# Value matmuls of two neighbouring query tiles in one TensorE visit, with the global keys' part as 32-row tiles

## The chip, the core and the metric

The kernel runs on one core of one Trainium2 chip. The metric is the device time of one execution in microseconds, as the median of several runs; smaller is better. A profile of one execution is read beside it. In the profile PE is TensorE, PEld its weight loads, DVE is VectorE, ACT is ScalarE, POOL is GpSimd and SP is SyncE, whose queue issues nearly all DMAs.

## What is computed

A sparse attention is followed by a feed-forward layer. There are 8 batches of 8 heads with a head size of 64. Each batch has 512 local queries and 32 global ones. A local query sees the 32 global keys and the local keys within 32 positions; a global query sees everything. The attention's 8 x 544 rows of 512 go through a two-layer network with an inner width of 2048 and an ELU between.

```python
s_g = scale * np.matmul(q_g, k_all.transpose(0, 1, 3, 2))        # global queries, all keys
out_g = np.matmul(sm(s_g), v_all)
mask = np.abs(pos[:, None] - pos[None, :]) <= window             # window = 32
s_ll = np.where(mask, s_ll, -1000000000.0)
s_l = np.concatenate([s_lg, s_ll], axis=-1)                      # global keys, local keys
a_l = sm(s_l)
out_l = np.matmul(a_l, np.concatenate([v_g, v_l], axis=2))
...
h = x @ w_in
g = np.where(h > 0.0, h, alpha * (np.exp(np.minimum(h, 0.0)) - 1.0))
return (g @ w_out).astype(np.float32)
```

## The kernel before

**Two streams on one core.** `attention()` and `ffn_stream()` are Python generators, and the loop at L858 interleaves them while the program is written out. Each `yield` of the attention is one step. `pace` (L845, from the table PACE) says how many chunks of the feed-forward layer stand in front of a step: none in the first 66 steps (the lead), about four a step up to step 112, about three a step after. A chunk is six matmuls of 256 columns in 16-bit parts. Work written with `defer(n, fn)` comes n ticks later, a tick being a chunk or a step without one. A planner then orders each engine's instructions by its own estimate of when they can run, taking program order as priority; waits and buffers are set by it.

**Attention.** A batch has two groups g of four heads and four tiles t of 128 local queries. The list `slots` has for each batch one slot "g" per group (global queries' scores, `stage_ga`) and eight slots "l" (g, t), in the order of two neighbouring tiles of group 0, then of group 1, and so on. In iteration i of L823 four steps are made, in the order S, V, T, U: S scores slot i (`stage_s`), V is `stage_v` of slot i - 3, T and U are `stage_t` and `stage_u` of slot i - 2. T transposes the softmaxed local scores of four heads into PSUM and copies them into `ptw` (two buffers, alternating); U transposes the scores against the global keys and copies them into `ptg` (one buffer for tile 0, another for all other tiles), and it copies the transposed scores of the global queries beside the local ones.

**The value matmuls (`stage_v`, L748).** For each of four heads three float32 matmuls add up in PSUM: the global keys (L767, 160 columns, the weights being `vG`, which holds the head's 32 global values in its own 32 rows of 128 and zeros elsewhere), and two windows of local keys (L769 and L771, 96 columns each). Two heads share the columns of one PSUM bank, on its lower and upper 64 partitions; both pairs of heads of one tile lie in one bank. A float32 matmul is two records in the trace, so that a visit has 24. After it ScalarE copies the local queries' part to `xr` (L775); one tick later VectorE adds the global queries' part to `xglob` (L780 for tile 0, L782 otherwise) and takes the maximum of the 256 new columns of `xr` (L784). When a block of 256 tokens is complete it is put into `ready`, and `split_x` cuts it into two 16-bit halves for the feed-forward layer.

**PSUM.** There are eight banks: `ps_h` two, `ps_o` two, `ps_a` four. The lead's V uses `ps_h`; later V, and S (two banks), `stage_ga` (two), T, U and `all_max` all use `ps_a`. Once the feed-forward layer has turned to its seven-product form (`ffn2_seven`, L398), that form keeps two banks of `ps_o`, one of `ps_h` and one of `ps_a` (L401 to L403) to the end, so that the attention has three banks of `ps_a` left, and `ffn1` one of `ps_h`.

**Loads.** All go through SP's queue in the program's order. `loads(i + 2)` is issued at the top of iteration i; for an "l" slot it brings q once and the tile's values `v` (384 KB, three buffers), for a "g" slot qg and k. A load into a buffer that is still read holds up the loads queued behind it.

Of the kernel before, what the change touches and what calls it, by code (L numbers as in the profile page):

```python
# [10 lines left out]
F32 = mybir.dt.float32  # L11
# [3 lines left out]
ALU = mybir.AluOpType  # L15
AX = mybir.AxisListType
# [6 lines left out]
P = 128  # L23
NT = SL // P
# [7 lines left out]
NP = NFT // 2  # L32
LAG2 = 2
LAGT, LAGV = 2, 3
AHEAD = 2


# [6 lines left out]
NX = 4  # L44
# [9 lines left out]


@with_exitstack
def attn_ffn(ctx: ExitStack, tc: tile.TileContext, qT, qgT, kT, vT, w_in, w_out, mask, out):
    nc = tc.nc
    scale = 1.0 / math.sqrt(D)

# [40 lines left out]
    make_identity(nc, ident)  # L101


    ptw = [wts.tile([P, 2, 4 * (HQ + 32) + 32], F32, name=f"ptw{i}") for i in range(2)]
# [186 lines left out]
    def ffn_stream():  # L291
# [203 lines left out]
        def split_x(blk):  # L495
            xr, mx = ready[blk]
            xh = ffn.tile([P, NC, BLK], F16, name="xh", bufs=NX)
            xl = ffn.tile([P, NC, BLK], F16, name="xl", bufs=NX)
            done = []
            xf, hf, lf = (a.rearrange("p c t -> p (c t)") for a in (xr, xh, xl))  # L500

            def s1():
                all_max(mx[:, 1:2], mx[:, 0:1])

            def s2():
                nc.vector.tensor_scalar_max(mx[:, 1:2], mx[:, 1:2], LOW)
# [12 lines left out]
            return xh, xl, mx, done  # L519
# [75 lines left out]


    def new_x():
        return ffn.tile([P, NC, BLK], F32, name="xr", bufs=3), ffn.tile([P, 10], F32, name="xm", bufs=NX + 4)

    xglob, mglob = wts.tile([P, NC, BLK], F32, name="xglob"), wts.tile([P, 10], F32, name="mglob")  # L600

    def attention():
        np_ = [0]
# [12 lines left out]
        def load_qg(b, g):  # L616
            qg = apool.tile([P, 2, SG], F32, name="qg", bufs=1)
            nc.sync.dma_start(qg, qgT[b, g])
            return qg

        def load_v(b, g, t):
            v = apool.tile([P, 12, D], F32, name="v", bufs=3)
            nc.sync.dma_start(v, vT[b, g, t])
            return v

# [110 lines left out]
        def stage_t(st, g, t):  # L736

            n = tiles[0]
            tiles[0] += 1
            pt, pz = st["pt", g, t] = ptw[n % 2], ptg[t == 0]  # L740
            tp = ps_a.tile([P, 512], F32, name="pa")
            for h in range(4):
                nc.tensor.transpose(tp[:, h * P:(h + 1) * P], st["p", g, t][:, h, 0:P], ident)  # L743
            copy = nc.vector.tensor_copy if "f" in tab or lead[0] else nc.scalar.copy
            copy(pt[:, :, 32:].rearrange("p a (h x) -> p a h x", h=4)[:, :, :, 0:HQ],
                 tp.rearrange("p (h a q) -> p a h q", h=4, a=2))

        def stage_v(st, g, t):  # L748

            half = t // 2  # L750
            blk = 2 * st["b"] + half
            if (g, t % 2) == (0, 0):
                st["x", half] = new_x()
            xr, mx = st["x", half]
            v = st["v", g, t]
            pt, pz = st["pt", g, t]
            if lead[0]:
                pv = ps_h.tile([P, 2, BLK], F32, name="h").rearrange("p a b -> p (a b)")
            else:
                pv = ps_a.tile([P, 512], F32, name="pa")  # L760
            for j in range(2):
                for i in range(3):
                    for r in range(2):
                        h = 2 * j + r
                        at = j * PW
                        if i == 0:
                            w, x, o = v[:, 8 + h, :], pz[:, 0:GW], slice(at, at + GW)  # L767
                        elif i == 1:
                            w, x, o = v[:, h, :], pt[:, 0, 32 + 96 * h:128 + 96 * h], slice(at, at + 96)  # L769
                        else:  # L770
                            w, x, o = v[:, 4 + h, :], pt[:, 1, 96 * h:96 + 96 * h], slice(at + HQ, at + GW)  # L771
                        nc.tensor.matmul(pv[64 * r:64 * r + 64, o], w, x, start=i == 0, stop=i == 2)  # L772
            pv = pv[:, 0:2 * PW].rearrange("p (j a x) -> p j a x", j=2, a=2)
            xt = xr[:, 2 * g:2 * g + 2, t % 2 * P:(t % 2 + 1) * P]
            nc.scalar.copy(xt.rearrange("p j (a x) -> p j a x", a=2), pv[:, :, :, 0:HQ])  # L775
            xg = xglob[:, 2 * g:2 * g + 2, st["b"] * SG:(st["b"] + 1) * SG]

            def out():
                if t == 0:
                    nc.vector.tensor_copy(xg, pv[:, :, 0, HQ:])  # L780
                else:
                    nc.vector.tensor_add(xg, xg, pv[:, :, 0, HQ:])  # L782
                i = 6 + 2 * g + t % 2
                nc.vector.tensor_reduce(out=mx[:, i:i + 1], in_=xt, op=ALU.max, axis=AX.XY, apply_absolute_value=True)  # L784
                if g == 1 and t == NT - 1:
                    i = 6 + st["b"] // 2
                    if st["b"] % 2:
                        c = slice((st["b"] - 1) * SG, (st["b"] + 1) * SG)
                        nc.vector.tensor_reduce(out=mglob[:, i:i + 1], in_=xglob[:, :, c], op=ALU.max, axis=AX.XY,
                                                apply_absolute_value=True)  # L790
                if g == 1 and t % 2 == 1:
                    ready[blk] = xr, mx
                    if blk == NBL - 1:
                        ready[NBL] = xglob, mglob

            defer(1, out)
# [85 lines left out]
def _layout(q_l, k_l, v_l, q_g, k_g, v_g, moe_w_in, moe_w_out):  # L882
# [8 lines left out]
    vG = np.zeros((B, H, NT, 4, 32, D), f)  # L891
    klT = k_l.transpose(0, 1, 3, 2)
    mask = np.zeros((P, 3, KW), f)
    neg = f(-8.0e9)
    for t in range(NT):
        for h in range(H):
            vG[:, h, t, h % 4] = v_g[:, h]
        for half in range(2):
            o = t * P + half * HQ
            own, left, right = range(o, o + HQ), range(o - 32, o), range(o + HQ, o + HQ + 32)  # L900
# [1 line left out]
            for c, key in enumerate([*own, *left, *right] if half == 0 else [*left, *right, *own]):  # L902
                if 0 <= key < SL:
# [7 lines left out]
    vT = np.concatenate([vW.reshape(B, 2, 4, NT, 2, P, D).transpose(0, 1, 3, 5, 4, 2, 6).reshape(B, 2, NT, P, 8, D),  # L911
                         vG.reshape(B, 2, 4, NT, P, D).transpose(0, 1, 3, 4, 2, 5)], axis=4)
    return dict(qT=qT, qgT=qgT, kT=kT, vT=vT, w_in=moe_w_in.view(np.int64), w_out=moe_w_out.view(np.int64), mask=mask)


# [15 lines left out]
```

## Time and profile before

| What | Value |
|---|---|
| median of 3 runs | 975.65 us (973.0 to 975.77) |
| span of the profiled execution | 972.1 us |
| ACT busy | 688.8 us (71%) |
| POOL busy | 261.9 us (27%) |
| bytes moved by DMA | 95.10 MB |
| value loads `v` | 64 of 384.0 KB |

The span is that of the profiled execution between its first and last instruction; the runs are timed from outside it, and the lowest of them, 973.0 us, is 0.9 us longer. The profile's busy time of an engine is the time in which at least one of its instructions was open. Matmuls are pipelined: a record of 0.27 us stands for a matmul that starts 0.11 us after the one before it, so the cost of a matmul is read from the distance between starts and not from a record's length.

### The profile page before, as it was taken

To read this page: it belongs to the slowest core of one execution; us is meant where nothing else is said; L and a number is where in the kernel's file an instruction comes from. 1 tells how busy PE (TensorE), PEld (TensorE's weight loads), DVE (VectorE), ACT (ScalarE), POOL (GpSimd) and SP (SyncE) were. 2 spreads that over 40 slices of the span, in tenths; PEclk is the share of its full clock that TensorE was granted. 3 is DMA by queue.
4 is the path that set the end of the run, shared out by engine and by line. 5 is a ranking of instruction groups with operands and counts; after the bars stand their busy time and mean duration, and the time that the engine had idled before them with its cause. 6 is when DMAs were issued, how large, how long until landed. Compare 5 with 4: busy or idle time off the path is not lost.

```text
span 972.1 us, 23882 instructions
## 1 busy us (share of the span) xinstructions
PE 926.0 (95%) x9216; PEld 737.7 (76%) x9216; DVE 750.3 (77%) x2258; ACT 688.8 (71%) x1668; POOL 261.9 (27%) x484
## 2 busy tenths in 40 slices
PE   6689779989999999999999999999999999999997
PEld 3466546566666788888888888888888888888886
DVE  4889989899996878677777778687786777676665
ACT  4779868767666768676777778677767767676674
POOL 4555735624042211231223122122222211100000
PEclk9799999999999999999999999999999999999999
DMA  7657666562331124102410133112311111000000
GB/s 275 240 176 251 234 206 227 179 210 75 109 112 61 55 94 132 51 19 84 148 66 19 56 110 132 35 43 107 110 57 34 40 34 40 1 23 23 1 23 22
DMA packets 39369, 95.10 MB, mean 98 GB/s; under 512 B 5944, under 2 KB 6456, under 8 KB 39256
## 3 DMA queue, kind: packets, MB, share of 16 engines
q1 hardware_dynamic: 39064, 93.32, 28.2%
q8 instruction: 72, 1.18, 0.5%
q14 instruction: 41, 0.34, 0.1%
q10 hardware_dynamic: 144, 0.13, 0.0%
q0 software_dynamic: 48, 0.13, 0.0%
HBM read 78.36 MB, written 15.20 MB: 96 GB/s over the span
## 4 chain that ended last, share of the span: by engine, by line
PE 60%; DVE 18%; ACT 10%; issue 7%; DMA 4%; POOL 1%; SPq 0%; POOLq 0%; DVEq 0%; ACTq 0%
PE h L307 21%; PE acc L424 10%; PE pa L772 5%; PE h L424 5%; PE acc L382 4%; PE pa L702 3%; ACT p L720 3%; DVE gl L328 3%; PE pa L307 2%; PE pa L424 2%; PE pa L743 2%; DVE g L325 2%; DVE p L713 2%; PE pa L635 2%; DVE cu L260 1%
## 5 line engine op out<-in xcount | busy, mean ns | idle before, releaser
L307 PE MATMUL h<-xh,winh 128*128 128x256 f16 x992 | 271.7, 274 | 5.2 <-ACT hs L317 4.9
L307 PE MATMUL h<-xh,winl 128*128 128x256 f16 x992 | 271.0, 273 | 0.5 <-DVE winl L201 0.5
L307 PE MATMUL h<-xl,winh 128*128 128x256 f16 x992 | 271.2, 273 | 0.0
L307 PEld LDWEIGHTS <-winh 128*128 128x128 f16 x2176 | 208.8, 98 | 47.0 <-issue 16.1
L727 POOL TENSOR_SCALAR p<-p,sm 128x128 f32<-128x128 f32 x256 | 124.7, 505 | 374.7 <-DVE sm L725 142.3
L325 DVE SCALAR_TENSOR_TENSOR g<-g,hs 128x512 f32<-128x512 f32 x136 | 95.7, 704 | 98.4 <-ACT g L318 97.9
L424 PEld LDWEIGHTS <-gh 128*128 128x128 f16 x1456 | 139.2, 98 | 23.6 <-issue 6.1
L720 ACT ACTIVATE p<-p,m 128x160 f32<-128x160 f32 x256 | 106.3, 418 | 60.6 <-DVE m L716 59.8
L307 PEld LDWEIGHTS <-winl 128*128 128x128 f16 x1088 | 106.8, 98 | 14.4 <-DVE winl L201 1.0
L328 DVE SCALAR_TENSOR_TENSOR gl<-gs,xs,gh 128x640 f16<-128x640 f32 x104 | 93.2, 897 | 26.0 <-ACT gh L347 25.8
L316 ACT ACTIVATE g<-h,xs 128x512 f32<-128x512 f32 x124 | 84.9, 685 | 37.2 <-PE h L307 36.8
L347 ACT ACTIVATE gh<-gs,xs 128x640 f16<-128x640 f32 x104 | 86.3, 829 | 34.4 <-DVE gs L343 34.4
L346 ACT ACTIVATE gh<-g,xs 128x256 f16<-128x256 f32 x104 | 53.1, 511 | 59.9 <-DVE g L325 59.0
L424 PE MATMUL acc<-wouth,gh 128*128 128x256 f16 (+1 forms) x312 | 88.0, 282 | 0.2 <-ACT gh L347 0.2
L318 ACT ACTIVATE g<-g 128x512 f32<-128x512 f32 x136 | 85.7, 630 | 0.1
L424 PE MATMUL acc<-wouth,gl 128*128 128x256 f16 x312 | 85.1, 273 | 0.2 <-DVE gl L328 0.2
L424 PE MATMUL acc<-woutl,gh 128*128 128x256 f16 x312 | 85.0, 273 | 0.0
L317 ACT ACTIVATE hs<-h,xs 128x512 f32<-128x512 f32 x124 | 84.5, 682 | 0.0
L424 PEld LDWEIGHTS <-gl 128*128 128x128 f16 x728 | 71.2, 98 | 12.9 <-DVE gl L328 0.5
L328 DVE SCALAR_TENSOR_TENSOR gl<-g,xs,gh 128x256 f16<-128x256 f32 (+1 forms) x136 | 75.4, 554 | 3.5 <-ACT gh L332 3.5
L713 DVE CUSTOM_DVE_ANT_0 p<-pa,msk 128x160 f32<-128x160 f32 x228 | 61.7, 316 | 0.9 <-PE pa L702 0.9
L664 POOL TENSOR_SCALAR pk<-pu,sg 32x32 f32<-32x32 f32 x64 | 41.0, 640 | 66.4 <-ACT gh L347 24.5
(219 smaller groups left out, 2020.2 us busy)
## 6 DMA issues: line engine op xcount, KB each, us to landing
v<-vT SPq DMA_DIRECT2D x64, 384.0 KB, 3.2
k<-kT SPq DMA_DIRECT2D x32, 640.0 KB, 5.1
q<-qT SPq DMA_DIRECT2D x32, 256.0 KB, 5.5
raw<-w_in SPq DMA_DIRECT2D x8, 1024.0 KB, 6.5
raw<-w_out SPq DMA_DIRECT2D x8, 1024.0 KB, 5.4
out<-o SPq DMA_DIRECT2D x32, 256.0 KB, 2.3
od<-o SPq DMA_DIRECT2D x24, 256.0 KB, 3.7
o<-od SPq DMA_DIRECT2D x24, 256.0 KB, 3.2
```

The lines of the kernel that those rows point to most:

```text
L307: nc.tensor.matmul(h[:, j, :], wt[:, c, f], xt[:, c, :], start=k == 0, stop=k == 11)
L316: nc.scalar.activation(g, hf, AF.Relu, scale=sc[:, p:p + 1])
L317: nc.scalar.activation(hs, hf, AF.Copy, scale=sc[:, 2 * NP + 1 + p:2 * NP + 2 + p])
L318: nc.scalar.activation(g, g, AF.Exp, scale=-1.0)
L325: nc.vector.scalar_tensor_tensor(out=g, in0=g, scalar=-1.0, in1=hs, op0=ALU.add, op1=ALU.max)
L328: nc.vector.scalar_tensor_tensor(out=dst, in0=src, scalar=sg, in1=hi, op0=ALU.mult, op1=ALU.subtract)
L346: nc.scalar.activation(gh[:, 0:2, :], two, AF.Copy, scale=sg)
L347: nc.scalar.activation(gh[:, 2:7, :], s, AF.Copy, scale=sg)
L424: nc.tensor.matmul(cols, gt, w, start=first, stop=last and k == len(todo) - 1)
L713: nc.vector.tensor_tensor_reduce(out=p, in0=sp[r][:, j * KW:(j + 1) * KW], in1=msk[:, mi, :], op0=ALU.add, op1=ALU.max, scale=1.0, scalar= ...
L720: nc.scalar.activation(ps[i], ps[i], AF.Exp, bias=m[:, 1, i:i + 1], scale=scale, accum_out=s[:, 0, i:i + 1])
L727: nc.gpsimd.tensor_scalar(ps[i][:, 0:P], ps[i][:, 0:P], s[:, 1, i:i + 1], 1.0, ALU.mult, ALU.mult)
```

## The change

`stage_v` is called for odd tiles only and computes two neighbouring tiles (s = 0 and 1) at once. It takes two PSUM banks, one for each pair of heads; the two tiles stand side by side in a bank. First come the global keys' matmuls of both tiles, as tiles of 32 rows: head h uses rows 32h to 32h+32 of the array, with the compact values `vg` of the batch in place of `vG`, and writes 128 columns (160 for tile 0, which has the global queries' own columns). Then come the 16 local matmuls, as before.

After it ScalarE makes two copies of 256 columns; VectorE sums the global queries' part over the two tiles with a `tensor_reduce` for each bank and takes one maximum over 512 columns. The second half's sum goes to a small tile `xg` that is added to `xglob` once a batch. `ptg` alternates with `ptw` and is no longer cleared at the start. `v` is 256 KB in four buffers, loaded at the top of its own slot's iteration, behind the other loads; `vg` (32 KB) is loaded once a group in the "g" slot. In `split_x` a maximum over four columns becomes one of two columns.

```diff
-    ptg = [wts.tile([P, PW], F32, name=f"ptg{i}") for i in range(2)]
+    ptg = [wts.tile([P, PW], F32, name=f"ptg{i}") for i in range(NPT)]
...
-    for p in (*ptg, *pkd):
+    for p in pkd:
         nc.gpsimd.memset(p, 0.0)
...
-            nc.vector.tensor_reduce(out=mx[:, 0:1], in_=mx[:, 6:10], op=ALU.max, axis=AX.X)
+            nc.vector.tensor_max(mx[:, 0:1], mx[:, 6:7], mx[:, 7:8])
...
+        def load_vg(b, g):
+            vg = apool.tile([P, D], F32, name="vg", bufs=3)
+            nc.sync.dma_start(vg, vgT[b, g])
+            return vg
+
         def load_v(b, g, t):
-            v = apool.tile([P, 12, D], F32, name="v", bufs=3)
+            v = apool.tile([P, 8, D], F32, name="v", bufs=4)
...
-            pt, pz = st["pt", g, t] = ptw[n % 2], ptg[t == 0]
+            pt, pz = st["pt", g, t] = ptw[n % NPT], ptg[n % NPT]
...
-        def stage_v(st, g, t):
+        def stage_v(st, g, half):
...
             if lead[0]:
-                pv = ps_h.tile([P, 2, BLK], F32, name="h").rearrange("p a b -> p (a b)")
+                pv = [ps_h.tile([P, 2, BLK], F32, name="h").rearrange("p a b -> p (a b)") for _ in range(2)]
             else:
-                pv = ps_a.tile([P, 512], F32, name="pa")
+                pv = [ps_a.tile([P, 512], F32, name="pa") for _ in range(2)]
+            vg = st["vg", g]
+            for s, t in ((1, ts[1]), (0, ts[0])):
+                pz = st["pt", g, t][1]
+                for h in (2, 3, 0, 1):
+                    j, r = divmod(h, 2)
+                    rows = slice(32 * h, 32 * h + 32)
+                    o, x = pv[j][64 * r:64 * r + 64, s * PW:(s + 1) * PW], pz[rows, :]
+                    if t == 0:
+                        o, x = o[:, 0:GW], x[:, 0:GW]
+                    else:
+                        o, x = (y.rearrange("p (a x) -> p a x", a=2)[:, :, 0:HQ] for y in (o, x))
+                    nc.tensor.matmul(o, vg[rows, :], x, start=s == 1, stop=False, skip_group_check=True)
+            for s, t in ((1, ts[1]), (0, ts[0])):
+                v, pt = st["v", g, t], st["pt", g, t][0]
+                for j in (1, 0):
+                    for i in range(2):
+                        for r in range(2):
+                            h = 2 * j + r
+                            at = s * PW + HQ * i
+                            x = pt[:, 0, 32 + 96 * h:128 + 96 * h] if i == 0 else pt[:, 1, 96 * h:96 + 96 * h]
+                            nc.tensor.matmul(pv[j][64 * r:64 * r + 64, at:at + 96], v[:, 4 * i + h, :], x,
+                                             start=False, stop=(s, i) == (0, 1), skip_group_check=True)
...
             for j in range(2):
-                for i in range(3):
...
-            nc.scalar.copy(xt.rearrange("p j (a x) -> p j a x", a=2), pv[:, :, :, 0:HQ])
-            xg = xglob[:, 2 * g:2 * g + 2, st["b"] * SG:(st["b"] + 1) * SG]
+                xt = xr[:, 2 * g + j, :]
+                nc.scalar.copy(xt.rearrange("p (s a x) -> p s a x", s=2, a=2), pv[j][:, :, :, 0:HQ])
+            xg = st["xg", half]

             def out():
-                if t == 0:
-                    nc.vector.tensor_copy(xg, pv[:, :, 0, HQ:])
-                else:
-                    nc.vector.tensor_add(xg, xg, pv[:, :, 0, HQ:])
-                i = 6 + 2 * g + t % 2
-                nc.vector.tensor_reduce(out=mx[:, i:i + 1], in_=xt, op=ALU.max, axis=AX.XY, apply_absolute_value=True)
...
+                for j in range(2):
+                    nc.vector.tensor_reduce(out=xg[:, 2 * g + j, :], in_=pv[j][:, :, 0, HQ:].rearrange("p s x -> p x s"),
+                                            op=ALU.add, axis=AX.X)
+                nc.vector.tensor_reduce(out=mx[:, 6 + g:7 + g], in_=xr[:, 2 * g:2 * g + 2, :], op=ALU.max, axis=AX.XY,
+                                        apply_absolute_value=True)
+                if g == 1:
+                    ready[blk] = xr, mx
+                if g == 1 and half == 1:
+                    nc.vector.tensor_add(st["xg", 0], st["xg", 0], xg)
...
                 st["qg", s[2]] = load_qg(s[1], s[2])
+                st["vg", s[2]] = load_vg(s[1], s[2])
...
-                st["v", s[2], s[3]] = load_v(s[1], s[2], s[3])
...
             if i + AHEAD < n:
                 loads(i + AHEAD)
+            load_values(i)
...
-                elif what == "V" and s2 and s2[0] == "l":
-                    stage_v(sts[s2[1]], *s2[2:])
+                elif what == "V" and s2 and s2[0] == "l" and s2[3] % 2 == 1:
+                    stage_v(sts[s2[1]], s2[2], s2[3] // 2)
```

More of the change, by code (lines that the diff above doesn't have):

```diff
@@ L34 @@
 LAGT, LAGV = 2, 3
+NPT = 2
 AHEAD = 2
@@ L56, in attn_ffn @@
 @with_exitstack
-def attn_ffn(ctx: ExitStack, tc: tile.TileContext, qT, qgT, kT, vT, w_in, w_out, mask, out):
+def attn_ffn(ctx: ExitStack, tc: tile.TileContext, qT, qgT, kT, vT, vgT, w_in, w_out, mask, out):
     nc = tc.nc
@@ L101, in attn_ffn @@
     make_identity(nc, ident)
-    ptw = [wts.tile([P, 2, 4 * (HQ + 32) + 32], F32, name=f"ptw{i}") for i in range(2)]
-    ptg = [wts.tile([P, PW], F32, name=f"ptg{i}") for i in range(2)]
+    ptw = [wts.tile([P, 2, 4 * (HQ + 32) + 32], F32, name=f"ptw{i}") for i in range(NPT)]
+    ptg = [wts.tile([P, PW], F32, name=f"ptg{i}") for i in range(NPT)]
     for p in ptw:
@@ L597, in new_x @@
     def new_x():
-        return ffn.tile([P, NC, BLK], F32, name="xr", bufs=3), ffn.tile([P, 10], F32, name="xm", bufs=NX + 4)
-    xglob, mglob = wts.tile([P, NC, BLK], F32, name="xglob"), wts.tile([P, 10], F32, name="mglob")
+        return ffn.tile([P, NC, BLK], F32, name="xr", bufs=3), ffn.tile([P, 8], F32, name="xm", bufs=NX + 4)
+    xglob, mglob = wts.tile([P, NC, BLK], F32, name="xglob"), wts.tile([P, 8], F32, name="mglob")
     def attention():
@@ L746, in stage_t @@
                  tp.rearrange("p (h a q) -> p a h q", h=4, a=2))
-        def stage_v(st, g, t):
-            half = t // 2
+        def stage_v(st, g, half):
             blk = 2 * st["b"] + half
-            if (g, t % 2) == (0, 0):
+            if g == 0:
                 st["x", half] = new_x()
+                st["xg", half] = (apool.tile([P, NC, SG], F32, name="xg", bufs=1) if half
+                                  else xglob[:, :, st["b"] * SG:(st["b"] + 1) * SG])
             xr, mx = st["x", half]
-            v = st["v", g, t]
-            pt, pz = st["pt", g, t]
+            ts = (2 * half, 2 * half + 1)
@@ L757, in stage_v @@
             if lead[0]:
-                pv = ps_h.tile([P, 2, BLK], F32, name="h").rearrange("p a b -> p (a b)")
+                pv = [ps_h.tile([P, 2, BLK], F32, name="h").rearrange("p a b -> p (a b)") for _ in range(2)]
             else:
-                pv = ps_a.tile([P, 512], F32, name="pa")
-            for j in range(2):
-                for i in range(3):
[L763 to L769, printed above, removed]
-                        else:
-                            w, x, o = v[:, 4 + h, :], pt[:, 1, 96 * h:96 + 96 * h], slice(at + HQ, at + GW)
-                        nc.tensor.matmul(pv[64 * r:64 * r + 64, o], w, x, start=i == 0, stop=i == 2)
@@ new lines, in stage_v @@
+            pv = [a[:, 0:2 * PW].rearrange("p (s a x) -> p s a x", s=2, a=2) for a in pv]
+            for j in range(2):
+                xt = xr[:, 2 * g + j, :]
+                nc.scalar.copy(xt.rearrange("p (s a x) -> p s a x", s=2, a=2), pv[j][:, :, :, 0:HQ])
+            xg = st["xg", half]
+            def out():
+                for j in range(2):
[7 more added lines that the diff above has]
+                    nc.vector.tensor_add(st["xg", 0], st["xg", 0], xg)
+                    if st["b"] % 4 == 3:
+                        i = 6 + st["b"] // 4
+                        c = slice((st["b"] - 3) * SG, (st["b"] + 1) * SG)
@@ L818, in loads, with load_values @@
                     nc.sync.dma_start(msk, mask)
-                st["v", s[2], s[3]] = load_v(s[1], s[2], s[3])
+        def load_values(i):
+            if 0 <= i < n and slots[i][0] == "l":
+                _, b, g, t = slots[i]
+                sts[b]["v", g, t] = load_v(b, g, t)
         for i in range(AHEAD):
@@ L890, in _layout @@
     vW = np.zeros((B, H, NT, 2, P, D), f)
-    vG = np.zeros((B, H, NT, 4, 32, D), f)
     klT = k_l.transpose(0, 1, 3, 2)
@@ L895, in _layout @@
     for t in range(NT):
-        for h in range(H):
-            vG[:, h, t, h % 4] = v_g[:, h]
         for half in range(2):
@@ L909, in _layout @@
     kT = kT.reshape(B, H // 2, P, NT, 2, KW)
[L911 to L913 removed]
+    vT = vW.reshape(B, 2, 4, NT, 2, P, D).transpose(0, 1, 3, 5, 4, 2, 6).reshape(B, 2, NT, P, 8, D)
+    vgT = v_g.reshape(B, 2, P, D)
+    return dict(qT=qT, qgT=qgT, kT=kT, vT=vT, vgT=vgT, w_in=moe_w_in.view(np.int64), w_out=moe_w_out.view(np.int64), mask=mask)
 def kernel(**inputs):
```

9 lines of the change are left out of this document (removed).

## The prediction

> **What bounds the kernel now.** I read the page's busy times and its 40 slices first, then the busy times by stretch, then what TensorE waited for.
>
> ```profile
> PE 926.0 (95%) x9216; PEld 737.7 (76%) x9216; DVE 750.3 (77%) x2258; ACT 688.8 (71%) x1668; POOL 261.9 (27%) x484
> PE   6689779989999999999999999999999999999997
> DVE  4889989899996878677777778687786777676665
> PE h L307 21%; PE acc L424 10%; PE pa L772 5%; PE h L424 5%; PE acc L382 4%; PE pa L702 3%; ACT p L720 3%; DVE gl L328 3%; PE pa L307 2%; PE pa L424 2%; PE pa L743 2%; DVE g L325 2%; DVE p L713 2%; PE pa L635 2%; DVE cu L260 1%
> ```
>
> ```profile
> 250.00:835.00 585.00, 581.84 (x6115) 480.73 (x6114) 446.13 (x1401) 420.45 (x1065) 130.49 (x262) 1.00 0.21 72
> 835.00:972.00 137.00, 130.69 (x1186) 115.58 (x1183) 91.00 (x205) 87.23 (x143) 5.96 (x10) 0.99 0.05 17
> 0.00:75.00 75.00, 55.39 (x636) 36.97 (x637) 51.90 (x251) 46.93 (x173) 39.37 (x90) 0.89 0.65 227
> 75.00:250.00 175.00, 158.13 (x1286) 104.43 (x1285) 161.29 (x404) 134.20 (x289) 86.04 (x122) 0.97 0.57 194
> ```
>
> The columns are the stretch, its length, then busy us of PE, PEld, DVE, ACT and POOL, the granted clock, the DMA share and GB/s. From 250 to 835 us TensorE is busy for 581.84 of 585 us, with DVE at 446 and ACT at 420. The waits of TensorE in that stretch, in total, number of times and longest, are one row:
>
> ```profile
> PE h L307 <- ACT hs L317: 2.8, 6, 0.9
> ```
>
> So there every microsecond of TensorE counts. From 75 to 250 us DVE is the busier engine (161 of 175) and TensorE has 17 us idle; in the lead (to 75 us) nothing is full and TensorE is busy for 74%. After 835 us no value matmul is left.
>
> **TensorE's part of the change.** The timeline of one V visit, with the feed-forward matmuls on either side (start, us, engine, line):
>
> ```profile
> 504.38 0.27 PE L424 MATMUL acc<-woutl,gh 128*128 128x256 f16 x1
> 504.49 0.27 PE L424 MATMUL acc<-wouth,gl 128*128 128x256 f16 x1
> 504.69 0.49 PE L772 MATMUL pa<-ptg,v 128*64 128x160 f32 x4
> 505.01 0.50 PE L772 MATMUL pa<-ptw,v 128*64 128x96 f32 x8
> 505.35 0.44 PE L772 MATMUL pa<-ptg,v 128*64 128x160 f32 x4
> 505.62 0.50 PE L772 MATMUL pa<-ptw,v 128*64 128x96 f32 x8
> 506.05 0.28 PE L424 MATMUL acc<-wouth,gh 128*128 128x256 f16 x1
> ```
>
> A neighbour takes 0.11 (504.38 to 504.49), so the visit costs 506.05 - 504.49 - 0.11 = 1.45 us. Eight 96-column records take 0.33 (505.01 to 505.35 is 0.34, with rounding), and as two column halves run side by side that is 0.083 a pair. Four 160-column records take 505.62 - 505.35 = 0.27, or 0.135 a pair. The first four take 0.32: 0.05 more, their first weight load. The way in costs 504.69 - 504.49 - 0.11 = 0.09, the way out 506.05 - 505.62 - 0.33 = 0.10. Check: 0.09 + 0.05 + 4 x 0.135 + 8 x 0.083 + 0.10 = 1.44.
>
> Do more than two float32 matmuls run at once? Two other visits tell, S with 64-row tiles, and the global queries' scores:
>
> ```profile
> 501.71 0.27 PE L307 MATMUL h<-xh,winl 128*128 128x256 f16 x1
> 501.92 0.78 PE L702 MATMUL pa<-k,q 64*64 64x160 f32 x16
> 502.62 0.28 PE L307 MATMUL h<-xh,winh 128*128 128x256 f16 x1
> ```
> ```profile
> 490.34 0.27 PE L424 MATMUL acc<-wouth,gl 128*128 128x256 f16 x1
> 490.54 0.66 PE L635 MATMUL pa<-k,qg 64*32 64x256 f32 x8
> ...
> 491.62 0.39 PE L424 MATMUL acc<-wouth,gh 128*128 128x512 f16 x1
> ```
> ```profile
> 507.59 0.27 PE L424 MATMUL pa<-raw,gl 128*128 128x256 f16 x1
> 507.70 0.60 PE L743 MATMUL pa<-ident,p 128*128 128x128 f32 x4
> 508.13 0.27 PE L307 MATMUL h<-xh,winh 128*128 128x256 f16 x1
> ```
>
> S has 16 records of 160 columns in 502.62 - 501.92 = 0.70. Less 0.05 and 0.10, that is 0.55 = 4 x 0.137: four at a time, in two row halves by two column halves. The 16 records of 256 columns at L635 and eight short ones take 1.08; two at a time they alone would take 8 x 0.216 = 1.73 (256/160 x 0.135 = 0.216), so four at a time too. The four transposes of 128 columns take 0.43, 0.108 each, and they show that a record of 128 columns costs 0.108.
>
> The new visit, for two tiles: in 0.09; 16 global records of 128 columns in four row groups, four at a time, 0.05 + 4 x 0.108 = 0.48; from 32-row to 128-row tiles once more a way in, 0.09 + 0.05 = 0.14; 32 local records, 16 pairs x 0.083 = 1.33; out 0.10. Sum 2.14, and 0.05 more for a pair with tile 0 (half of its global columns are 160 wide, 2 x 0.027), so 2.17 in the mean, against 2 x 1.45 = 2.90. **A pair saves 0.73.** The inner change of tile shape stands in no row: nothing or a whole way in and out (0.24) are its ends; I take the way in, since no 16-bit work follows.
>
> How many pairs lie where TensorE is the bound? The value line's busy time by stretch (PE, PEld, clock, DMA):
>
> ```profile
> 250.00:835.00 585.00, 64.09 (x1080) 55.63 (x1080) 1.00 0.21 72
> 0.00:75.00 75.00, 15.94 (x240) 13.30 (x240) 0.89 0.65 227
> ```
>
> 1080 / 24 = 45 visits, 22.5 pairs, x 0.73 = 16.4 us. In the lead ten visits: 0.73 / 2.90 = 25% of 15.94 = 4.0, of which I take half, 2.0, because TensorE is busy for 74% there, often behind the softmax. The other 64 - 55 = 9 visits, 4.5 pairs x 0.73 = 3.3, stand where DVE leads; I take a quarter, 0.8. Sum 19.2, with 16.4 and 23.7 as ends.
>
> **ACT, DVE, POOL.** ACT's copies keep their number and shape. DVE:
>
> ```profile
> L784 DVE TENSOR_REDUCE xm<-xr 128x1 f32<-128x256 f32 x64 | 26.1, 408 | 0.0
> L185 DVE TENSOR_REDUCE cm<-cu 128x1 f32<-128x1024 f32 x8 | 9.6, 1205 | 0.0
> L782 DVE TENSOR_TENSOR xglob<-xglob,pa 128x64 f32<-128x64 f32 x41 | 8.2, 200 | 0.7 <-ACT xr L775 0.7
> L686 DVE TENSOR_REDUCE ptg<-pa 128x32 f32<-128x128 f32 x16 | 4.5, 283 | 0.6 <-ACT ptg L683 0.5
> ```
>
> A pair cost 2 x (0.20 + 0.41) = 1.22. The maximum over 512 lies between L784 and L185: 0.41 + 256 x (1.205 - 0.408) / 768 = 0.67. A sum of 64 elements out of PSUM lies between 0.20 and 0.28, two of them 0.40 to 0.56. So 1.07 to 1.23, plus one small addition a batch (0.2 like L782) and an unchanged `split_x`: nothing, between -4 and +2 us of DVE over 32 pairs, hidden by its quarter of idle time after 250 us. The cleared `ptg` at the start was not waited for: nothing.
>
> **Loads.**
>
> ```profile
> v<-vT SPq DMA_DIRECT2D x64, 384.0 KB, 3.2
> SPq L623 <- PE pa L772: 298.1, 42, 20.5
> ```
>
> A third of `v` goes (64 x 128 KB), 16 loads of 32 KB come. SP's queue stood for 298.1 us behind value loads whose buffer was still read; q, k, weights and the output's loads and stores queue behind. With four buffers, loads two slots later and a visit that frees two at once, a load finds its buffer freed an iteration before, except one a batch that waits within its own iteration. A load has three iterations, some 30 us (835 us for 80 slots), for a landing of 3.2. I take nothing for it; a gain of some us in the lead, where DMA is busy for 65%, is the other end.
>
> **The added wait.** After 334 us three `ps_a` banks are left, since one holds the products below to the end:
>
> ```profile
> L424 PE MATMUL pa<-raw,gh x208: 272/273/283, 334.2 to 965.7; 128*128 128x256 f16 x104
> ```
>
> S or the global scores hold two when V comes, and V now wants two: it must wait until one is read. Behind it in TensorE's queue stand feed-forward matmuls, and behind those ACT and DVE. Two cases:
>
> ```profile
> 544.28 0.77 PE L702 MATMUL pa<-k,q 64*64 64x160 f32 x16
> 546.95 0.49 PE L772 MATMUL pa<-ptg,v 128*64 128x160 f32 x4
> ```
> ```profile
> 547.45 0.32 DVE L713 CUSTOM_DVE_ANT_0 p<-pa,msk 128x160 f32<-128x160 f32 x1
> ```
> ```profile
> 600.62 0.49 PE L772 MATMUL pa<-ptg,v 128*64 128x160 f32 x4
> 602.41 0.47 ACT L653 ACTIVATE pg<-pa,mg 128x256 f32<-128x256 f32 x1
> ```
>
> In the first, the second of four DVE reads (heads 0 and 2 of one bank) ends at 547.77, 0.82 after V started. In the second a bank of the global scores is free at 602.88, 2.26 after it. From 334 to 835 us stand some 19 pairs (22.5 x 501 / 585). Four of them follow a "g" slot, 4 x 2.26 = 9 us; two come when no S is left; 13 follow S, and at half of 0.82 they make 5. The ends are nothing, if the planner puts feed-forward matmuls ahead of V, and 14 us, if it never does. I take 3, near the lower end, since the row of waits (2.8 us) shows that its order has kept TensorE fed beside ACT and DVE chains of this length.
>
> Net: -19.2 + 3 = -16.2. The profiled span of 972.1 would be 955.9. The runs' median is 3.5 us above that span, and I keep this distance: 975.65 - 16.2 = **959.5 us**.
>
> **The rivals.**
> - *Two banks are not free.* The whole 14 us of waits come: -19.2 + 14 = -5.2, 970.5 us. For it speaks that three banks must carry S's two and V's two; against it that there are other matmuls to put ahead, and that all waits of TensorE in this stretch are 2.8 us now.
> - *Row groups that share a bank take turns.* Heads 2 and 3 write one bank from two row groups, 0 and 1 the other. In the order 2, 3, 0, 1 that makes three turns (2; 3 with 0; 1) for one: 2 x 4 x 0.108 = 0.86 more, the pair costs 0.13 more than before, x 27 = 3.5, with 3 of waits 982 us. Against it: at L635 the row halves r = 0 and 1 write the same bank `halves[i]` on different partitions, and ran four at a time. The Trainium skill, "TensorEngine Tiling (Array Packing)", "Restrictions and Gotchas", says that different row tiles cannot access one PSUM bank at the same time; by that rule this rival is the forecast. The rows of L635 do not agree with it for different partitions.
> - *32-row tiles run one at a time* (slower). Place: the 16 global records. 16 x 0.108 = 1.73 in place of 0.43, a pair +0.57, x 27 = 15, with 3 of waits 994 us. It decides once the global part passes 0.48 + 0.73 = 1.21 us. For it: no row has 32-row tiles. Against it: 64-row tiles overlap at L635 and L702.
> - *The work leaves TensorE, but the time stays*, since DVE or ACT become the bound: counting only the stretch after 330 us, where DVE has a quarter idle, 19 pairs x 0.73 = 14, less 3: 964.5 us. It lies within the forecast's range.
>
> **Chances.** Forecast 0.71 (951 to 967), the last rival 0.06 (inside it), banks 0.12 (967 to 975), turns 0.06, one at a time 0.05. A measurement can tell about 0.3%, 2.9 us. A third of the banks' rival and of the turns count as the same, for waits larger and smaller than priced: faster 0.71 + 0.06 + 0.08 = 0.85, same 0.06, slower 0.04 + 0.05 = 0.09. The range goes down to 949, where the upper end of lead and middle (23.7), an inner change of shape at nothing (27 x 0.14 = 3.8) and no waits meet (948), and up to 972, above the banks' rival; beyond it lie the turns, one at a time and the worst of the banks.
>
> **What would show it.** The distance from the last matmul before a visit to the first after it should be about 2.25 (2.14 and 0.11), with the first 16 records in some 0.5; 0.9 or more there is turns, 1.7 one at a time. A gap of over 0.25 inside it prices the change of shape. New rows of TensorE waiting for DVE L713 or ACT's reads of the global scores, in sum above 3 us, are the banks. DVE's busy time should stay within 4 us of 750.3. The value line's stretch from 250 us on should end some 16 us earlier and the 137 us after the attention stay as they are. The forecast is wrong if the lead loses time to the pair's later start, or if the planner moves the feed-forward stream.

## The result and the profile after

The changed kernel takes 983.72 us (median of 5 runs, 981.35 to 985.17) against 975.65: a ratio of 1.0088, with an interval from 1.0062 to 1.0114. It is slower by 8 us, where 959.5 was forecast. The profiled span is 981.6 us against 972.1.

The busy times of the changed kernel's page and the shares of the chain that ended last, then its stretches (columns as before):

```profile
PE 924.0 (94%) x9216; PEld 728.0 (74%) x9216; DVE 754.0 (77%) x2232; ACT 690.2 (70%) x1668; POOL 274.5 (28%) x482
PE 42%; DVE 29%; ACT 18%; issue 8%; POOL 2%; DMA 1%; POOLq 0%; SPq 0%; ACTq 0%; DVEq 0%
```
```profile
0.00:75.00 75.00, 55.01 (x557) 33.77 (x557) 48.08 (x221) 41.70 (x153) 31.71 (x79) 0.80 0.59 205
75.00:250.00 175.00, 159.77 (x1354) 105.75 (x1347) 162.22 (x422) 136.59 (x304) 97.63 (x131) 0.97 0.55 185
250.00:835.00 585.00, 569.06 (x6017) 464.54 (x6015) 446.91 (x1375) 417.89 (x1058) 139.22 (x262) 1.00 0.19 64
835.00:982.00 147.00, 140.22 (x1301) 123.94 (x1298) 96.76 (x216) 94.00 (x156) 5.94 (x10) 0.99 0.05 16
```

The third row is the one to see. In the stretch that was full before (581.84 of 585 us), TensorE is now idle for 16 us: about what the change was to save, but as holes in the stretch and not as its end. DVE and ACT are as busy as before. TensorE's waits there, which were one row of 2.8 us, are now:

```profile
PE h L308 <- ACT hs L318: 5.8, 11, 1.0
PE pa L778 <- DVE m L719: 4.6, 5, 1.8
PE pa L778 <- ACT pg L659: 3.7, 4, 1.6
PE acc L383 <- DVE o L391: 1.0, 1, 1.0
PE pa L778 <- ACT ptg L689: 0.2, 1, 0.2
```

L778 is the new visit's first matmul. It waits for DVE to read the local scores (L719) or for ACT to read the global ones (L659): for banks of `ps_a`. L308 is the first feed-forward matmul of a group, which waits for ACT to read its `h` bank.

**What a visit costs.** The timeline of a visit that nothing holds up:

```profile
736.25 0.27 PE L308 MATMUL h<-xh,winl 128*128 128x256 f16 x1
736.45 0.67 PE L778 MATMUL pa<-ptg,vg 32*64 32x128 f32 x16
737.04 1.54 PE L787 MATMUL pa<-ptw,v 128*64 128x96 f32 x32
738.52 0.28 PE L308 MATMUL h<-xh,winh 128*128 128x256 f16 x1
```

It costs 738.52 - 736.25 - 0.11 = 2.16 us for two tiles; 2.14 was forecast. The 32-row part, with the change of tile shape, takes 737.04 - 736.45 = 0.59, forecast 0.48 + 0.14. So 32-row tiles do run four at a time. Another visit:

```profile
495.72 0.27 PE L425 MATMUL pa<-raw,gl 128*128 128x256 f16 x1
495.92 0.65 PE L778 MATMUL pa<-ptg,vg 32*64 32x128 f32 x8
496.50 0.88 PE L787 MATMUL pa<-ptw,v 128*64 128x96 f32 x16
497.31 0.28 PE L308 MATMUL h<-xh,winh 128*128 128x256 f16 x1
...
497.87 0.27 PE L308 MATMUL h<-xh,winl 128*128 128x256 f16 x1
498.62 0.65 PE L778 MATMUL pa<-ptg,vg 32*64 32x128 f32 x8 [0.48 <-ACT pg L659]
499.20 0.88 PE L787 MATMUL pa<-ptw,v 128*64 128x96 f32 x16
500.02 0.28 PE L308 MATMUL h<-xh,winh 128*128 128x256 f16 x1
```

The planner has split this visit: two heads of both tiles first, the other two after six feed-forward matmuls, and the second half still waits until ACT has read the global scores' bank. Eight 32-row records take 0.58, as long as 16 in the whole visit; that fits two row groups running where four could. The first half costs 497.31 - 495.72 - 0.11 = 1.48 us, as much as a visit of the kernel before; the second 2.04, with a wait.

**Where the time went.** The same distances, summed over all visits between the 26th and the 64th copy into `xr` (19 pairs of tiles; 335.1 to 834.7 us before, 337.5 to 844.8 after), with what feed-forward matmuls that follow each other take above 0.11 us each (0.22 for 512 columns):

| us in this stretch | V | T and U | feed-forward above its rate |
|---|---|---|---|
| before | 55.0 | 26.7 | 4.4 |
| after | 57.0 | 28.7 | 8.6 |

V was to fall by 13.9 and rises by 2.0; 2.0 and 4.2 come in the other columns, together 8.2. The stretch itself is 7.7 us longer (507.3 against 499.6), so the columns account for it to half a microsecond. Of the 9.5 us by which the spans differ, 2.4 had been lost ahead of it, where 5 were to be gained, and 0.6 are won back behind it.

Three of the 19 pairs are split as above; together they cost 4.6 us more than three visits that nothing holds up. Nine others have no feed-forward matmuls inside, but stop inside the visit, most of them after four records, where the second bank comes first into use. Eight of the nine wait there for L719 or L659; the longest, at 603 us, takes 4.74 us. They make the rest. Of the 6.2 us in the other columns, waits for ACT's read of `h` make about 3 (5.8 against 2.8 us by the rows), and matmuls at half the clock 1.7 (last section). The rest is not attributed.

### The profile page after: what moved, and what is told of

Read it like the earlier page. It is cut to its first block, busy times and chain, and to the rows that moved or that the text cites. A ratio compares the mean times of both kernels' runs of the same rounds, so it can differ in the third digit from the quotient of the medians.

```text
span 981.6 us, 23874 instructions
## 1 busy us (share of the span) xinstructions
PE 924.0 (94%) x9216; PEld 728.0 (74%) x9216; DVE 754.0 (77%) x2232; ACT 690.2 (70%) x1668; POOL 274.5 (28%) x482
## 4 chain that ended last, share of the span: by engine, by line
PE 42%; DVE 29%; ACT 18%; issue 8%; POOL 2%; DMA 1%; POOLq 0%; SPq 0%; ACTq 0%; DVEq 0%
PE h L308 15%; PE acc L425 7%; DVE g L326 4%; ACT p L726 3%; DVE gl L329 3%; PE h L425 3%; DVE p L719 3%; PE pa L787 3%; ACT g L317 3%; PE pa L308 2%; ACT hs L318 2%; ACT g L319 2%; PE pa L708 2%; PE pa L749 2%; PE acc L383 2%
## 5 line engine op out<-in xcount | busy, mean ns | idle before, releaser
L308 PE MATMUL h<-xh,winh 128*128 128x256 f16 x992 | 272.6, 275 | 9.5 <-ACT hs L318 8.9
L308 PE MATMUL h<-xh,winl 128*128 128x256 f16 x992 | 272.1, 274 | 0.5 <-DVE winl L202 0.5
L308 PE MATMUL h<-xl,winh 128*128 128x256 f16 x992 | 272.3, 275 | 0.0
L308 PEld LDWEIGHTS <-winh 128*128 128x128 f16 x2176 | 210.2, 98 | 52.6 <-issue 21.3
L733 POOL TENSOR_SCALAR p<-p,sm 128x128 f32<-128x128 f32 x256 | 135.3, 545 | 375.7 <-DVE sm L731 204.7
L308 PEld LDWEIGHTS <-winl 128*128 128x128 f16 x1088 | 107.1, 98 | 15.4 <-DVE winl L202 1.1
L719 DVE CUSTOM_DVE_ANT_0 p<-pa,msk 128x160 f32<-128x160 f32 x228 | 61.7, 319 | 1.8 <-PE pa L708 1.8
L749 PE MATMUL pa<-ident,p 128*128 128x128 f32 x256 | 44.9, 291 | 11.6 <-POOL p L733 9.5
```

Source lines behind the costliest of these rows:

```text
L308: nc.tensor.matmul(h[:, j, :], wt[:, c, f], xt[:, c, :], start=k == 0, stop=k == 11)
L719: nc.vector.tensor_tensor_reduce(out=p, in0=sp[r][:, j * KW:(j + 1) * KW], in1=msk[:, mi, :], op0=ALU.add, op1=ALU.max, scale=1.0, scalar= ...
L733: nc.gpsimd.tensor_scalar(ps[i][:, 0:P], ps[i][:, 0:P], s[:, 1, i:i + 1], 1.0, ALU.mult, ALU.mult)
```

## The experiments

Two theories for the 8 us after 335 us. **Banks**: V's two banks are not free, and the splits and waits of V are the whole loss. **Burst**: a pair loads ACT and DVE in bursts, and ACT as a whole comes too late, whatever the banks. A third one, **loads**, is for the lead, which ended at 79.3 us (the tenth copy into `xr`) against 73.2. Each run was timed in five rounds beside the kernel before, which had medians of 974.83 to 975.24 in them.

| Kernel | us | ratio to before, 95% interval |
|---|---|---|
| b_free | 982.08 | 1.0073 [1.0057, 1.0089] |
| a_free | 975.84 | 1.0009 [0.9998, 1.0020] |
| a_vtsu | 993.95 | 1.0190 [1.0171, 1.0208] |
| a_stvu | 974.34 | 0.9994 [0.9981, 1.0006] |
| b_hfree | 982.86 | 1.0074 [1.0054, 1.0094] |
| a_hfree | 982.67 | 1.0077 [1.0059, 1.0094] |
| b_free2 | 971.14 | 0.9959 [0.9945, 0.9972] |
| a_free2 | 961.97 | 0.9873 [0.9858, 0.9889] |
| a_oldloads | 982.20 | 1.0070 [1.0056, 1.0084] |
| b_newloads | 978.62 | 1.0029 [1.0010, 1.0047] |
| a_stvu_old | 973.26 | 0.9985 [0.9971, 0.9999] |
| b_strided | 971.60 | 0.9968 [0.9958, 0.9979] |

### One more bank for the attention, in both kernels

```diff
                 state["seven"] = [ps_o.tile(...), ps_o.tile(...),
-                                  ps_h.tile(...),
-                                  ps_a.tile([P, 512], F32, name="pa")]
+                                  ps_h.tile(...)]
+                state["seven"].append(state["seven"][0])
...
-                    nc.tensor.matmul(cols, gt, w, start=first, ...
+                    nc.tensor.matmul(cols, gt, w, start=first and i < 3, ...
```

> The kernel before, with the seventh product added into the first product's bank (its sums are wrong, its matmuls are as many), so that the attention keeps four ps_a banks to the end. All theories: it never lacked a bank, so 975 us within 4; every V visit stays at 1.45 us. It is the base for the same edit on the changed kernel.

> The changed kernel with the seventh product added into the first product's bank (same leaving out as in b_free), four ps_a banks to the end. Banks theory: what is lost after 334 us comes from V wanting two of three banks; no visit is split or waits, a pair costs 2.2 us, 19 pairs x 0.73 = 14 us less than b_free after 334 us, and with the lead's loss (5.5, of which the middle gives 3.4 back) about 13 us less than b_free, near 962. Burst theory (two ACT copies and the longer DVE work of a pair at once hold up the feed-forward layer whatever the banks): TensorE's waits for ACT hs stay near 6 us and the kernel stays within 3 us of b_free.

With the fourth bank no visit is split, and V falls from 55.0 us (b_free) to 41.6 in the stretch: 13.4, as the prediction's 0.73 a pair has it. But a_free is only 6.2 us below b_free, where 13 were expected. The edit itself costs b_free 6.8 us, which was not expected: with the shared bank TensorE waits for ACT (L433, 5.4 us), and a_free pays nearly as much (4.5 us). What a_free pays alone is the first row of its waits from 260 to 840 us, followed by the same row of b_free:

```profile
PE h L308 <- ACT hs L318: 8.2, 14, 1.0
```
```profile
PE h L307 <- ACT hs L317: 1.9, 4, 0.7
```

The 6.3 us more of these waits are most of the 7.2 that a_free falls short of V's 13.4. So the bank shortage is one limit, worth 57.0 - 41.6 = 15.4 us of V, and another stands right behind it.

### Another order of the steps

```diff
-            for what in "SVTU":
+            for what in "SVTU" if lead[0] else "VTSU":
```

> The changed kernel with the four steps of an iteration in the order V, T, S, U once the lead is over, so that two steps lie between S and V on either side and S's banks are read before V wants them. Nothing is left out. Banks theory: the splits and V's waits after 334 us go (11 us), and with them the 4.7 us of waits for ACT hs and the 1.6 us at half clock: 983.7 - 17 = 966 us. Burst theory: the waits for ACT hs stay, 975 or more. If S now waits for V's banks in V's place, nothing is gained, 983.

A miss: 10 us slower than the changed kernel. No visit after the lead's end was short of a bank, and none of TensorE's waits is for L719 or L659. But V now comes right behind the U that writes its `ptg`, and waits for ACT's copy:

```profile
PE pa L778 <- ACT ptg L689: 25.9, 21, 2.1
PE h L308 <- ACT hs L318: 4.4, 9, 0.8
```

With S, T, V, U there are two steps on that side too. T then writes a `ptw` that V has not read, so a third buffer is needed:

```diff
-            pt, pz = st["pt", g, t] = ptw[n % NPT], ptg[n % NPT]
+            pt, pz = st["pt", g, t] = ptw[0], ptg[n % NPT]
+            ptw.append(ptw.pop(0))
...
+            if len(ptw) == 2 and len(added) == NP:
+                p = ffn.tile([P, 2, 4 * (HQ + 32) + 32], F32, name="cu", bufs=3)
...
+                ptw.insert(0, p)
-            for what in "SVTU":
+            for what in "SVTU" if len(ptw) == 2 else "STVU":
```

> The changed kernel with the steps in the order S, T, V, U from the point (about 330 us) where the weights' sums are done; a third ptw buffer, needed since T now comes ahead of V, takes the place of a buffer of those sums. Nothing is left out. In the run with V, T, S, U the bank waits went, but V came right behind U and waited 25.9 us for ACT's copy into ptg; here S and T lie between U and V, and T between S and V. Banks theory: no visit split, no wait of V, 11 us of V and 1.6 us at half clock gone: 983.7 - 12.6 = 971 us. What is left of the missing gain is the wait of the feed-forward layer for ACT's read of its one h bank (about 6 us), which this does not touch. If the wait only moves again: 980 or more.

974.34 is 9.4 us faster than the changed kernel, and 3.3 us above the 971 that the banks theory gave. V takes 47.7 us in the stretch and no visit is split, but V still waits behind the global scores (DVE mg, and 1.5 us for ACT pg), so it does not come down to the 41.6 of a_free. The waits for ACT's read of `h` stay (260 to 840 us):

```profile
PE h L308 <- ACT hs L318: 6.6, 13, 1.3
PE pa L779 <- DVE mg L655: 1.8, 2, 1.2
```

So the loss is undone without a bank more, but there is no gain over the kernel before: V is 7.3 us shorter than in that kernel, and T, U and the feed-forward matmuls are 8.6 longer.

### The wait for ACT

Where do these waits stand? In both kernels every one of them after 250 us (6 before, 11 after) lies between two groups of first-layer matmuls with no V visit between them. In the changed kernel they come 14 to 26 us after the start of the last V visit, in the iterations without one. TensorE, then ACT (an "ACTIVATION_READ_ACCUMULATOR" row left out between the others), at the longest:

```profile
488.15 0.27 PE L681 MATMUL pa<-ident,pz 128*128 128x128 f32 x1
489.30 0.27 PE L308 MATMUL h<-xh,winh 128*128 128x256 f16 x1 [0.88 <-ACT hs L318]
```
```profile
485.62 0.69 ACT L317 ACTIVATE g<-h,xs 128x512 f32<-128x512 f32 x1 [0.46 <-PE h L308]
486.92 0.43 ACT L726 ACTIVATE p<-p,m 128x160 f32<-128x160 f32 x1 [0.62 <-DVE m L722]
...
488.58 0.67 ACT L318 ACTIVATE hs<-h,xs 128x512 f32<-128x512 f32 x1
```

ACT reads `h` twice, and between the two reads it waited 0.62 us for DVE and did four softmax exponentials (486.92 to 488.58). Since its last first-layer matmul TensorE had done 21 second-layer matmuls, a T visit and a transpose of U, and no V stood there to fill the rest. It needed `h` 0.88 us too soon. No `xr` copy is in the way. That is the cushion theory of the next expectation: a V visit between two groups had given ACT the time. Two `h` banks would take this wait away:

```diff
                 state["seven"] = [ps_o.tile(...), ps_o.tile(...),
-                                  ps_h.tile(...),
                                   ps_a.tile([P, 512], F32, name="pa")]
+                state["seven"].append(state["seven"][0])
...
-                    nc.tensor.matmul(cols, gt, w, start=first, ...
+                    nc.tensor.matmul(cols, gt, w, start=first and i < 3, ...
```

> The changed kernel with the seventh product added into the first one's bank (its sums are wrong, its matmuls as many), and the bank that this sets free given to the first feed-forward matmuls (two h banks, three ps_a banks). Cushion theory: in iterations without a V visit nothing stands between two groups of the first feed-forward matmuls, and TensorE waits for ACT to read the single h bank; with two banks its waits for ACT hs after 260 us (5.8 us here, 8.2 in a_free) go to below 1, while the bank waits of V (V 52.7 us after 337 us) stay as in the changed kernel. Against b_hfree then 2 to 5 us more is lost than against it in a_free. Burst theory: the waits are for ACT as a whole and stay above 4.

> The kernel before with the same edit as a_hfree (the seventh product in the first one's bank, two h banks), as its base. It waits for ACT hs 2.8 us only after 258 us, so 1 to 3 us below b_free's 982.1.

The waits for ACT hs go to nothing in both, so they were for the one `h` bank. V, short of banks as in the changed kernel, is at 54.0 us against 55.0. The two kernels are level (982.67 and 982.86): against its base a_hfree stands 6.0 us worse than a_free did, where 2 to 5 were expected. b_hfree, expected 1 to 3 us below b_free, is not faster than it. The shared bank is in the way of more (a_hfree waits 9.9 us for ACT's L434, b_hfree 6.9). So TensorE still waits for ACT, at another bank: these two don't price the wait cleanly, and they don't rule out the burst theory. The next edit keeps two `h` banks and avoids that wait:

```diff
-                state["seven"] = [ps_o.tile(...), ps_o.tile(...), ps_h.tile(...), ps_a.tile(...)]
+                state["seven"] = [ps_o.tile(...), ps_o.tile(...)] * 2
...
-                    nc.tensor.matmul(cols, gt, w, start=first, ...
+                    nc.tensor.matmul(cols, gt, w, start=first and i < 2, ...
...
-                    elif i < 3:
-                        nc.scalar.activation(e[i]..., acc[i], AF.Copy, scale=oc)
+                    elif i == 2:
+                        for m in (0, 2):
+                            nc.scalar.activation(e[m]..., acc[m], AF.Copy, scale=oc)
+                    elif i == 3:
+                        nc.scalar.activation(e[1]..., acc[1], AF.Copy, scale=oc)
```

> The kernel before with four products of the seven added into the banks of the others, two banks in all (the sums are wrong, the matmuls as many; ACT reads the shared banks after the last product, so that nothing waits for it in between). The attention keeps four ps_a banks and the first feed-forward matmuls two h banks. V stays at 1.45 us a visit, 55 us after 335 us; the waits for ACT hs (2.8 us) go: 971 to 975.

> The changed kernel with the same edit as b_free2: four ps_a banks and two h banks to the end. If the missing gain is bank waits of V (15 us) plus waits for ACT's read of the one h bank (6 us) and nothing else, then V falls from 55 to 41.6 us after 335 us, no wait takes its place, and with 1.9 us before it the kernel ends 13 to 16 us below b_free2, near the 959.5 that was predicted. If a third limit stands behind these two (DVE or ACT as a whole), it stays within 8 us of b_free2, as a_free did of b_free (6.2).

With both limits lifted in both kernels the change gains 9.2 us (961.97 against 971.14). b_free2 has no wait of TensorE left from 260 to 840 us, and the rows for ACT hs and for V's banks are gone in a_free2. ACT has the same work and the pairs are the same, and yet TensorE waits for ACT for only 3.4 us in all, so the burst theory falls here. The largest waits left are:

```profile
PE acc L423 <- ACT o L436: 1.9, 2, 1.1
PE acc L383 <- DVE o L391: 1.0, 1, 1.0
PE pa L779 <- ACT ptg L690: 1.0, 3, 0.6
```

V falls by 12.6 (55.0 to 42.4), and 4.5 of it come back in small pieces: 0.8 in T and U, 2.9 between feed-forward matmuls, 0.8 at `all_max`. 13 to 16 us were expected; the missing 4 to 7 are these and the 1.9 us that were counted ahead of 335 us, of which nothing is left there.

### The lead and the loads

```diff
                 if i == 1:
                     nc.sync.dma_start(msk, mask)
+                st["v", s[2], s[3]] = load_v(s[1], s[2], s[3])
...
-            load_values(i)
```

> The changed kernel with the value loads issued two iterations ahead, in the old place in SP's queue. Loads theory: in the lead SP is no longer held by value loads, so the first w_out load starts at 13.35 us instead of 22.03 and its conversion crowds the softmax on DVE; with the old place the lead's last copy comes at about 73 us instead of 78.7, and the end 2 to 5 us earlier. Pair theory: the lead is late since a pair starts only when its second tile is transposed; then the lead stays at 78 and the end within 2 us of the changed kernel.

The lead ended at 75.4 us, and the median is 1.5 us lower, though the two kernels' runs overlap. But the mechanism is not the one that was expected: the first `w_out` load starts early even so (13.35 us in the changed kernel).

```profile
13.98 0.66 SPq L160 DMA_DIRECT2D raw<-w_out  x1
```

The other way round, the kernel before with its value loads behind the others (`load_values(i - 1)`, three buffers):

> The kernel before with its value loads issued at the top of the iteration after their slot's, behind the other loads (three buffers as before), so that they hold up nothing in SP's queue. Loads theory: the lead ends later, by up to 4 us (the changed kernel's lead ended at 79.3 us, 75.4 with the old place), as the weight loads come earlier and their conversion crowds DVE. Whether that reaches the end: in the changed kernel undoing it was worth 1.5 us, so 975 to 979 here.

978.62, slower by 0.1 to 0.5%: the `w_out` load starts at 12.01 us instead of 22.03, the lead ends at 75.4, and the 20th copy into `xr` comes at 263.0 us instead of 258.1. So in the kernel before the place of the loads matters, by 1 to 5 us; the path by which it does is not shown. In the changed kernel the 1.5 us are not clear of the scatter. The two edits together:

> The changed kernel with the steps in the order S, T, V, U from about 330 us (a third ptw buffer) and the value loads two iterations ahead in the old place. The two edits alone gave 974.3 and 982.2 against 983.7; if they add, 973; if the loads matter only within the scatter of the lead, 974 to 975.

973.26 against 974.34 for one of them, which is inside the scatter of the runs.

Over all executions with the changed lead its end came at 74.8 to 79.3 us, over those with the old one at 70.6 to 75.8, and by the 26th copy into `xr` (334.4 to 337.5, and 335.1 to 340.1) there is no difference. Why the changed lead is late is left open.

### A version that beats both

```diff
                         if i == 0:
                             w, x, o = v[:, 8 + h, :], pz[:, 0:GW], slice(at, at + GW)
+                            if t:
+                                nc.tensor.matmul(pv[...].rearrange("p (a x) -> p a x", a=2)[:, :, 0:HQ], w,
+                                                 pz.rearrange("p (a x) -> p a x", a=2)[:, :, 0:HQ], start=True, stop=False, ...)
+                                continue
```

> The kernel before with one thing taken out: for tiles other than 0 the global keys' matmul streams 128 columns in place of 160, leaving out the 32 between that only tile 0 needs. 4 x 0.027 = 0.11 us a visit less, three quarters of 45 visits after 250 us: 3.7 us, and some of the rest. No bank more, the same cushion. By the price of a column 971.5 us; if any shortening of V only exposes ACT's read of h, within 1 us of before.

971.60: 3.3 us below the kernel before, as the price of a column has it, and 12 below the changed kernel. A visit of these tiles costs 1.34 instead of 1.45, V 51.9 instead of 55.0 us in the stretch, and the waits for ACT hs from 260 to 840 us are 3.7 against 2.8. Each visit kept its place, its one bank and its time ahead of `h`.

## Why the prediction was wrong

- **What bounds the kernel**: right. TensorE bounds it from 250 to 835 us, and 0.11 us off three visits in four came out at the end as 3.3 us, where their sum gives 3.7 (b_strided).
- **The price of a visit**: right. 2.16 to 2.22 against 2.14 to 2.19, 13.4 us in 19 pairs against 13.9 (a_free). The inner change of shape, estimated at 0.14, comes to 0.11, if the 32-row matmuls take the 0.48 they were put at.
- **Turns, or one at a time**: neither. Four row groups, two to a bank on different partitions, ran at once: the 32-row part took 0.59 us, and by the prediction's estimate turns would have added 0.86 to it. The rule that the prediction named from the Trainium skill, "TensorEngine Tiling (Array Packing)", "Restrictions and Gotchas", that different row tiles cannot access one bank at the same time, does not agree with these rows, and the measurement decides.
- **The added wait**: this step failed. It had the place right and a range of nothing to 14 us, and took 3, near the lower end, because the planner could put feed-forward matmuls ahead. Measured: 15.4 us in V (57.0 against 41.6). The matmuls that could be put ahead did not cover the wait: nine visits stopped inside, and three were split. Two halves at 1.48 us without a wait cost 2.96, as much as the two old visits (2.90), so a split alone uses up a pair's saving. That TensorE waited only 2.8 us before was no evidence for a wait that had not existed.
- **ACT costed at nothing**: this failed too. ACT's work is the same, but the prediction did not ask what gave ACT its time. The V visits, one for each query tile, had been the cover: in the iterations that now have none TensorE reaches the one `h` bank before ACT has read it. These waits rose from 2.8 to 5.8 us, and with a bank for V to 8.2 (a_free, 1.9 in its base). They are about half of the 6.2 us that T, U and the feed-forward matmuls took more.
- **The lead, the middle and the 2.5 us from 250 to 335 us** (5 us together): nothing was left of them at 335 us. In the profiled executions the changed kernel is 2.4 us late there; over all runs the two leads show no difference at that point.
- **The rivals**: the banks were there at 970.5 us with 0.12. Their sign came true (8.3 us of new waits for L719 and L659, where more than 3 were to show it), and 14 us was near the 15.4. What kept this rival's time too low is what it shared with the forecast: no price for what a missing V visit uncovers, and a gain ahead of 335 us that did not come.
- **Sum**: V's saving after 335 us (13.9) was given back by the banks, with 2.0 on top. 6.2 more were lost in T, U and the feed-forward matmuls, about half of it in waits for `h`, and the 5 us ahead of the stretch did not come. That is 8 us slower by the medians.

## What to carry over

A step that wants two buffers of a pool at once must be counted against the pool at the moment it runs: list who holds each bank then and how long after its last matmul it is read. A planner that fills the gap does not remove the shortage; it may cut the step in two. And when TensorE's work is taken out of some iterations, look at which reader of a single-buffered bank that work had been giving time to. A small saving spread over all iterations can be worth more than a large one in half of them.

## What was not expected of the hardware

After a visit that waited 1.62 us in its middle TensorE ran at half its clock for a while. Its records and the granted clock of the 5 us from 607 us (third column from the end, 0.66):

```profile
606.45 0.65 PE L778 MATMUL pa<-ptg,vg 32*64 32x128 f32 x8 [1.62 <-ACT pg L659]
...
608.37 0.42 PE L308 MATMUL h<-xh,winl 128*128 128x256 f16 x1
608.59 0.42 PE L308 MATMUL h<-xh,winh 128*128 128x256 f16 x1
```
```profile
607.00:612.00 5.00, 5.00 (x42) 3.86 (x41) 2.05 (x6) 1.23 (x4) 2.51 (x5) 0.66 0.38 111
```

From 608.2 to 611.4 us neighbours stand 0.21 apart, not 0.11, which costs 1.7 us, as much again as the wait. That the wait brought it on is not shown: a visit at 767.28 us waited 1.79 us, and the matmuls after it stand 0.11 apart. In the lead (to 75 us) the granted clock is 0.80, against 0.89 before. Whether that makes the lead late was not tried. Six kernels with the same lead had 0.76 to 0.84 there, and the latest end, 79.3 us, came with 0.80, while the three with 0.76 ended at 77.3 to 77.7.
